# First layer's first block in whole float32 products; its weights are split later, for the second block

## Chip, core and metric

The kernel runs on one core of a Trainium2 chip. The metric is the device time of one execution in microseconds (us). TensorE (PE) multiplies, VectorE (DVE) and ScalarE (ACT) do the elementwise work, GpSimd (POOL) does almost nothing, and SyncE (SP) issues nearly all transfers.

## What is computed

A linear attention with a complex decay over 768 positions (4 batches, 8 heads of 48), and behind it two layers of a feed-forward network over 3072 tokens of 384 features, with 2048 hidden features each. The input of the first layer is the attention's output.

```python
for t in range(S):
    new_re = ar * S_re - ai * S_im
    new_im = ar * S_im + ai * S_re
    S_re, S_im = (new_re + k[t] ⊗ v[t], new_im)
    y[t] = q[t] · S_re
h = x @ w_in;  g = max(h, 0) + log1p(exp(-|h|));    x = g @ w_out     # first layer
h = x @ w_in2; g = h * tanh(softplus(h));           out = g @ w_out2  # second layer
```

## The kernel before

**Work.** The tokens are 24 units of 128. For each unit the attention runs through a decay path, sums over the positions (products with the triangular `mask`, the tiles `cum` and `pa`), a `trig` step and `heads`. Three units form a block of 384 tokens of the first layer; there are 8 such blocks, and 6 blocks of 512 in the second layer. A block goes through 16 slots, one for each chunk `f` of 128 hidden features. In the text slots 0 to 15 are the first block, 16 to 31 the second.

**Split numbers.** The products are made in the form float32r. Each operand is held as a high and a low part, and each product is made three times: high by high, low by high, high by low. The input `x` of a block gets its parts in `heads` (ACT writes the high one, DVE the low one). A slot of the first layer (`mlp`) makes nine products into the PSUM tile `h` (three pieces of 128 features, three times each), then g in eight elementwise steps on ACT and DVE (tiles `rt`), splits g into `rhi` (a cast) and `rlo` (a subtraction on DVE), and `products` makes nine products more, three into each of three accumulators `acc`.

**Weights.** `w_prep` brings one chunk of raw 64-bit numbers into a ring of two buffers (`wr`; the first two chunks have buffers in `x`), puts float32 together in four elementwise passes, casts the high part into the tile `w` and subtracts for the low part. The 16 chunks are prepared before and during the first block, each ahead of the slot that needs it, and stay for all eight blocks. Then the second layer's chunks replace them.

**Order.** A planner in the kernel (`Recorder.schedule`) takes each operation's priority (`prio`, in slots) and a cost and writes one fixed order for each engine. Operations of the kind `Flex` may go to DVE or ACT, and the planner picks which; so a change at one place moves others. `warm` fills gaps that the planner sees on PE up to the slot `WARM` = 7 with filler products of `mask` by itself (tile `idle`), at first all gaps, from slot 0 on those above 1.5 us.

Of the kernel before, what the change touches and what calls it, by code (L numbers as in the profile page):

```python
# [17 lines left out]
DM = H * D  # L18
# [411 lines left out]
class Engine:  # L430
# [16 lines left out]
    def cost(self, method, k):  # L447
        if method == "preload_act_table_set":
            return 1.283, 0.0
        out = k.get("out")  # L450
        n = out.size() if isinstance(out, View) else 0
        if method == "dma_start":
            v = min((v for v in (out, k["in_"]) if isinstance(v, View)), key=lambda v: v.size())
            return (1.0 if self.name == "pool" else 0.62), max(v.size() * 4 * (v.box[0][1] - v.box[0][0]) / 350e3, 0.5)
        if self.name == "act":
            ps = any(isinstance(v, View) and v.h.pool.psum for v in k.values())
            wide = any(isinstance(v, View) and v.h.dt == I32 for v in k.values())
            return (0.00094 if wide else 0.000833) * n + (0.051 if ps else 0.093) + (0.093 if "accum_out" in k else 0.0) + (0.093 if isinstance(k.get("bias"), View) else 0.0), 0.0
        if self.name == "dve":
            ps = any(isinstance(v, View) and v.h.pool.psum for v in k.values())  # L460
            fast = method in ("tensor_scalar", "tensor_copy") and not ps
            return (0.00052 if fast else 0.00104) * n + 0.068, 0.0
        if self.name == "pool" and method == "copy":
            return 0.00107 * n + 0.07, 0.0
        if self.name == "pool":
            return 0.0023 * n + 0.07, 0.0
        if self.name == "pe":
            rhs = k["rhs"].size()
            if k["rhs"].h.dt == F32R:
                return max(0.000414 * rhs + 0.0143, 0.107), 0.0  # L470
            if rhs == 128 and k["lhsT"].size() <= 64:
                return 0.116, 0.0
            if rhs > 128:
                return 0.001684 * rhs, 0.0
            if rhs <= 64:
                return 0.167, 0.0
            return 0.223, 0.0
        raise AssertionError(method)


def emit(tc, ri, qk, vp, w1, w2, outT, fit):
# [46 lines left out]
    def f32(v):  # L528
        return v.bitcast(F32)
# [21 lines left out]
    pool.memset(out=hpi, constant=math.pi / 2)  # L551


    W = {}


    spare = {}
    for u, f in GUESTS.items():
        spare[u] = {}
        for i, part in enumerate(PARTS):  # L560
            w, o = wp.tile((P, 4, DM), F32, f"w{f - i}"), 0
            for tag, n in part:
                spare[u][tag] = w[:, o:o + n] if n > 1 else w[:, o]
                o += n

    def w_prep(layer, f, prio, raw=None):
        rec.prio = prio
        w = wp.tile((P, 2, 2 * DM), F32R, f"w{f}")
        if raw is None:
            raw = ring1.tile((P, 2 * DM, 2), I32, "wr", bufs=WR)  # L570
        sp.dma_start(out=raw.rearrange("p b t -> p (b t)"), in_=(w1, w2)[layer - 1][f].bitcast(I32))
        lw, hw = raw[:, :, 0], raw[:, :, 1]
        wact.scale(out=f32(hw), in_=f32(hw), scale=2.0 ** -112)
        av.top3(out=lw, in_=lw)
        dve.scalar_tensor_tensor(out=lw, in0=hw, scalar=-(2 ** 31), in1=lw, op0=ALU.bitwise_and, op1=ALU.bitwise_or)
        dve.scalar_tensor_tensor(out=lw, in0=hw, scalar=3, in1=lw, op0=ALU.logical_shift_left, op1=ALU.bitwise_or)
        avp.copy(out=w[:, 0], in_=f32(lw))
        vp2.tt(out=w[:, 1], in0=f32(lw), in1=f32(w[:, 0]), op=ALU.subtract)
        for i, kind in enumerate("io"):
            W[layer, kind, f] = (w[:, 0, i * DM:(i + 1) * DM], w[:, 1, i * DM:(i + 1) * DM])  # L580


    unit_blk = {}
# [94 lines left out]
    def heads(u, t, ed, cs):  # L678
# [74 lines left out]
            xblk[j] = ring1.tile((P, NJ + 1, 2, 3 * P), F32R, "x", 2)  # L753
        x = xblk[j]
        o = slice(i0 * P, (i0 + 1) * P)
        act.activation(out=x[:, :, 0, o], in_=y, func=AF.Copy, accum_out=flags[:, u, 3:4])
        dve.tensor_tensor(out=x[:, :, 1, o], in0=y, in1=f32(x[:, :, 0, o]), op=ALU.subtract)
        if i0 == BLOCKS1[j] - 1:
            for i in range(6):
                s0 = 16 * i if i < 3 else 64 + 16 * (i - 3)  # L760
                d0 = 48 + 64 * (i % 2)
                sp.dma_start(out=f32(x[d0:d0 + 16, i // 2, :, 0:nb]), in_=f32(x[s0:s0 + 16, NJ, :, 0:nb]))


    class Slot:
# [19 lines left out]

    def mlp(s):
        n = s.n
        hi, lo = W[s.layer, "i", s.f]
        x = xblk[s.j] if s.layer == 1 else x2blk[s.j]
        rec.prio = s.i  # L790
        h = ps.tile((P, 512), F32, "h", BANKS)[:, 0:n]
        with rec.group("pe"):
            k = 0
            for wt, xi in ((hi, 0), (lo, 0), (hi, 1)):
                for j in range(NJ):
                    mm(h, wt[:, j * P:(j + 1) * P], x[:, j, xi, 0:n], k == 0, k == 8)
                    k += 1
        if chain:
            rec.ops[-1].extra = (chain.pop(),)
        chain.append(rec.ops[-1])  # L800
        rec.prio = s.i - L_ELEMENTWISE
        if s.layer == 1:
            t1, t2 = rt(s, "t1", 3), rt(s, "t2", 2)
            av.abs(out=t1, in_=h)
            act.activation(out=t1, in_=t1, func=AF.Exp, scale=-1.0)

            act.activation(out=t2, in_=t1, func=AF.Identity, bias=1.0)
            dve.scalar_tensor_tensor(out=t2, in0=t2, scalar=1.0, in1=t1, op0=ALU.subtract, op1=ALU.subtract)
# [12 lines left out]
        dve.tensor_scalar(out=z, in0=hs, scalar1=20.0, scalar2=None, op0=ALU.min)
        act.activation(out=z, in_=z, func=AF.Exp)
        act.activation(out=z, in_=z, func=AF.Ln, scale=0.5, bias=1.0)
        dve.tensor_tensor(out=z, in0=z, in1=hs, op=ALU.add)
        batch.append((s, hs, z))
        if len(batch) < VISIT:
            return
        rec.prio = s.i - L_VISIT
        with rec.group("act"):
            act.preload_act_table_set("sigmoid_and_others")  # L830
            for _, _, z in batch:
                act.activation(out=z, in_=z, func=AF.Sigmoid)
            act.preload_act_table_set("natural_log_exp_and_others")
        for r, g, z in batch:
            rec.prio = r.i - L_GATE
            ghi, glo = rt(r, "hi", 4, F32R), rt(r, "lo", 4, F32R)
            dve.tensor_tensor(out=g, in0=g, in1=z, op=ALU.mult)
            av.copy(out=ghi, in_=g)
            dve.tensor_tensor(out=glo, in0=g, in1=f32(ghi), op=ALU.subtract)
            products(r, ghi, glo)  # L840
        batch.clear()

    def products(s, ghi, glo):
        n = s.n
# [6 lines left out]
        for e in range(NJ):  # L851
            o = slice(e * P, (e + 1) * P)
            with rec.group("pe"):
                mm(a[e][:, 0:n], hi[:, o], ghi, first, False)
                mm(a[e][:, 0:n], lo[:, o], ghi, False, False)
                mm(a[e][:, 0:n], hi[:, o], glo, False, last)
            if last:
                if s.layer == 1:
                    t = rt(s, "ev", 2)
                    av.copy(out=t, in_=a[e][:, 0:n])  # L860
                    sp.dma_start(out=x2d[e, :, s.t0:s.t0 + n], in_=t)
                else:
# [318 lines left out]
```

## Time and profile before

| | us |
|---|---|
| median of 3 runs (1054.78 to 1057.41) | 1055.84 |
| the profiled execution's own time | 1053.35 |
| its span from first to last instruction | 1051.6 |
| first product of slot 0 | 64.2 |
| first product of slot 16 | 160.3 |
| first product of slot 32 | 233.7 |
| PE busy in the span | 1017.9 |
| DVE busy | 921.5 |
| ACT busy | 875.3 |

A busy time is the union of an engine's records. The records of PE are longer than the distance between two products, since a product starts while the one before it is still in the array, and the fillers count as busy too. The records of DVE and ACT overlap a little in the same way. So the text takes the cost of an instruction from the distance between two starts where it can.

### The profile page before, as it was taken

What the parts mean: (1) busy time and instruction counts of PE and PEld (TensorE: products, weight loads), DVE (VectorE), ACT (ScalarE), POOL (GpSimd) and SP (SyncE); (2) the same over time, 40 slices, a digit from 0 to 9 for tenths busy, and PEclk for the clock granted to TensorE, in tenths of its full rate; (3) what the DMA queues carried; (4) which work ended last, traced back from release to release, by engine and by line L of the source; (5) the groups of instructions that cost most, each with busy time, mean ns of one, the idle gap of its engine ahead of it and who ended that gap; (6) DMA issues with size and microseconds to landing.
All of it is one profiled execution on the core that took longest, in us unless ns stands there. A gap on an engine that the chain in (4) does not pass through costs nothing.

```text
span 1051.6 us, 17036 instructions
## 1 busy us (share of the span) xinstructions
PE 1017.9 (97%) x6022; PEld 911.3 (87%) x6022; DVE 921.5 (88%) x1680; ACT 875.3 (83%) x1639; POOL 16.4 (2%) x28
## 2 busy tenths in 40 slices
PE   9999879999999999999999999789999999999997
PEld 8898778999999999999999998568888888888886
DVE  7999999999999999999998999898877687776764
ACT  8987989889889888898986789659888877788883
POOL 0000000000000000000000000000000000000000
PEclk9999999999999999999999999899999999999999
DMA  6157453344434444444334323221010100000000
GB/s 265 46 162 215 148 162 89 81 94 100 94 83 99 98 86 95 86 98 97 68 73 102 112 94 112 90 91 41 21 31 31 30 31 1 1 31 1 31 1 33
DMA packets 158791, 84.69 MB, mean 81 GB/s; under 512 B 136916, under 2 KB 139988, under 8 KB 158696
## 3 DMA queue, kind: packets, MB, share of 16 engines
q1 hardware_dynamic: 158056, 83.45, 29.7%
q8 instruction: 49, 0.80, 0.3%
q14 instruction: 46, 0.38, 0.1%
q0 software_dynamic: 640, 0.06, 0.1%
HBM read 55.11 MB, written 9.50 MB: 61 GB/s over the span
## 4 chain that ended last, share of the span: by engine, by line
PE 81%; DVE 8%; ACT 6%; DMA 3%; issue 1%; SPq 0%; DVEq 0%; ACTq 0%
PE acc L986 34%; PE h L986 34%; PE pa L986 7%; PE cum L986 5%; DMA wr<-w 2%; DVE rt L992 2%; DVE wr L992 2%; ACT rt L992 1%; ACT L982 1%; PE idle L986 1%; ACT w L992 1%; DVE w L992 1%; DVE rlo L992 1%; ACT wr L966 0%; DMA w<-ri 0%
## 5 line engine op out<-in xcount | busy, mean ns | idle before, releaser
L986 PE MATMUL h<-x,w 128*128 128x384 f32 (+1 forms) x2016 | 435.9, 362 | 10.0 <-DVE w L990 6.2
L986 PEld LDWEIGHTS h<-x,w 128*128 128x128 f32 x2016 | 366.3, 190 | 47.4 <-DVE w L990 7.0
L992 ACT ACTIVATE rt<-rt 128x384 f32<-128x384 f32 (+1 forms) x672 | 361.0, 565 | 51.5 <-DVE rt L992 44.4
L986 PE MATMUL acc<-rhi,w 128*128 128x384 f32 (+1 forms) x1344 | 383.3, 366 | 3.2 <-ACT rhi L988 2.2
L986 PEld LDWEIGHTS acc<-rhi,w 128*128 128x128 f32 x1344 | 246.0, 189 | 34.2 <-ACT rhi L988 4.2
L986 PE MATMUL acc<-rlo,w 128*128 128x384 f32 (+1 forms) x672 | 242.5, 361 | 1.4 <-DVE rlo L992 1.3
L992 DVE TENSOR_TENSOR rt<-rt,rt 128x512 f32<-128x512 f32 (+1 forms) x320 | 196.9, 633 | 22.1 <-ACT rt L992 20.1
L982 ACT ACT_TABLE_LOAD x115 | 147.5, 1283 | 2.8 <-PEq L1164 0.8
L986 PEld LDWEIGHTS acc<-rlo,w 128*128 128x128 f32 x672 | 126.7, 188 | 15.9 <-DVE rlo L992 4.7
L992 DVE TENSOR_TENSOR rlo<-rt,rhi 128x384 fp32r<-128x384 f32 (+1 forms) x224 | 136.0, 610 | 4.6 <-ACT rhi L988 3.0
L988 ACT CAST rhi<-rt 128x384 fp32r<-128x384 f32 (+1 forms) x158 | 86.4, 548 | 28.0 <-DVE rt L992 21.4
L992 DVE SCALAR_TENSOR_TENSOR rt<-h,rt 128x384 f32<-128x384 f32 x128 | 69.0, 552 | 0.5
L992 DVE SCALAR_TENSOR_TENSOR rt<-rt,rt 128x384 f32<-128x384 f32 x128 | 68.6, 549 | 0.7 <-ACT rt L992 0.4
L992 DVE TENSOR_SCALAR rt<-rt 128x512 f32<-128x512 f32 x96 | 40.8, 426 | 29.9 <-ACT rt L988 28.4
L979 ACT ACTIVATE rt<-h 128x384 f32<-128x384 f32 x92 | 44.6, 486 | 21.3 <-DVE rlo L992 10.4
L992 DVE SCALAR_TENSOR_TENSOR wr<-wr 128x768 int32<-128x768 int32 x58 | 55.2, 956 | 1.0 <-ACT wr L966 1.0
L990 DVE COPY rt<-h 128x512 f32<-128x512 f32 x49 | 33.8, 690 | 23.9 <-PE h L986 23.3
L986 PE MATMUL pa<-qkT 96*128 96x128 f32 x384 | 49.1, 278 | 4.9 <-DVE qt L992 1.6
L986 PEld LDWEIGHTS pa<-qkT 96*128 96x128 f32 x384 | 46.4, 191 | 7.5 <-DVE qt L992 2.0
L988 ACT COPY rt<-h 128x512 f32<-128x512 f32 x47 | 27.5, 586 | 28.4 <-PE h L986 27.9
L986 PEld LDWEIGHTS idle<-mask 128*128 128x128 f32 x388 | 46.8, 198 | 3.6 <-DVE mask L990 1.7
L986 PE MATMUL idle<-mask 128*128 128x128 f32 x388 | 47.7, 282 | 1.7 <-DVE mask L990 1.7
(115 smaller groups left out, 985.8 us busy)
## 6 DMA issues: line engine op xcount, KB each, us to landing
wr<-w SPq DMA_DIRECT2D x29, 768.0 KB, 4.2
qkT<-st SPq DMA_DIRECT2D x252, 64.0 KB, 2.3
ri<-ri SPq DMA_DIRECT2D x22, 384.0 KB, 3.1
qkin<-qk SPq DMA_DIRECT2D x22, 384.0 KB, 3.5
v<-vp SPq DMA_DIRECT2D x24, 256.0 KB, 3.6
x2d<-rev SPq DMA_DIRECT2D x24, 192.0 KB, 2.1
x2r<-x2d SPq DMA_DIRECT2D x6, 768.0 KB
outT<-rev SPq DMA_DIRECT2D x18, 256.0 KB, 2.0
```

The lines of the kernel that those rows point to most:

```text
L979: eng.activation(out=o, in_=i, func=AF.Abs)
L982: eng.preload_act_table_set(*a)
L986: eng.matmul(res(k["out"]), lhsT=res(k["lhsT"]), rhs=res(k["rhs"]), start=k["start"], stop=k["stop"])
L988: eng.copy(res(k["out"]), res(k["in_"]))
L990: eng.tensor_copy(res(k["out"]), res(k["in_"]))
L992: getattr(eng, method)(*[res(v) for v in a], **{n: res(v) for n, v in k.items()})
```

## The change

In the first block neither x nor g is split, and a product is made once in whole float32, with whole weights: three products instead of nine into `h`, three instead of nine into `acc`. `w_prep` of the first layer ends with the whole chunk. A new function `split` makes the high and low parts from the whole chunk; it is called after each slot of the first block with a priority 8 slots before the slot of the second block that needs it. High and low parts have tiles of their own now, and the low part of chunk `f` takes the place of the whole chunk `f - 1`. The six transfers that complete x carry one part instead of two for the first block. The planner's cost of a product with `mask` seen as float32 rises with this.

```diff
+WHOLE = 16
+L_SPLIT = 8.0
...
-            if k["rhs"].h.dt == F32R:
+            if k["rhs"].h.dt == F32R and not any(c[0] == "bitcast" for c in k["rhs"].chain):
...
+        if layer == 1:
+            whole[f] = wp.tile((P, 2 * DM), F32, f"w{f}a")
+            dve.scalar_tensor_tensor(out=whole[f].bitcast(I32), in0=hw, scalar=3, in1=lw, op0=ALU.logical_shift_left, op1=ALU.bitwise_or)
+            return
         dve.scalar_tensor_tensor(out=lw, in0=hw, scalar=3, in1=lw, op0=ALU.logical_shift_left, op1=ALU.bitwise_or)
-        avp.copy(out=w[:, 0], in_=f32(lw))
-        vp2.tt(out=w[:, 1], in0=f32(lw), in1=f32(w[:, 0]), op=ALU.subtract)
+        split(layer, f, f32(lw))
+
+    def split(layer, f, w):
+
+        hi = wp.tile((P, 2 * DM), F32R, f"w{f}b")
+        lo = wp.tile((P, 2 * DM), F32R, f"w{f - 1}a" if f else "w")
+        avp.copy(out=hi, in_=w)
+        vp2.tt(out=lo, in0=w, in1=f32(hi), op=ALU.subtract)
...
-        act.activation(out=x[:, :, 0, o], in_=y, func=AF.Copy, accum_out=flags[:, u, 3:4])
-        dve.tensor_tensor(out=x[:, :, 1, o], in0=y, in1=f32(x[:, :, 0, o]), op=ALU.subtract)
+        if NF * j < WHOLE:
+            act.activation(out=f32(x[:, :, 0, o]), in_=y, func=AF.Copy, accum_out=flags[:, u, 3:4])
...
+            if s.i < WHOLE:
                 for j in range(NJ):
-                    mm(h, wt[:, j * P:(j + 1) * P], x[:, j, xi, 0:n], k == 0, k == 8)
-                    k += 1
+                    mm(h, whole[s.f][:, j * P:(j + 1) * P], f32(x[:, j, 0, 0:n]), j == 0, j == NJ - 1)
...
+            if s.i < WHOLE:
+                g = rt(s, "hi", 2, F32R)
+                dve.tensor_tensor(out=f32(g), in0=t1, in1=t2, op=ALU.add)
+                products(s, g, None)
+                return
...
+                if glo is None:
+                    mm(a[e][:, 0:n], whole[s.f][:, DM + e * P:DM + (e + 1) * P], f32(ghi), first, last)
...
+        if WHOLE - NF <= s.i < WHOLE:
+            rec.prio = s.i + NF - L_SPLIT
+            split(1, s.f, whole[s.f])
```

The order on DVE around the elementwise work of the first two slots, before (`rt` are the temporaries of g, `td`, `xs`, `qt` and `st` belong to the attention):

```order
L992 SCALAR_TENSOR_TENSOR rt_734<-h,rt_734 128x384
L992 SCALAR_TENSOR_TENSOR rt_765<-rt_765,rt_739 128x384
L992 TENSOR_TENSOR rt_698<-rt_698,rt_734 128x384
L992 SCALAR_TENSOR_TENSOR rt_765<-h,rt_765 128x384
L990 CAST rhi<-rt_698 128x384
L992 TENSOR_TENSOR td<-ri 128x384
L992 TENSOR_TENSOR rlo<-rt_698,rhi 128x384
L977 TENSOR_SCALAR rt_866<-h 128x384
```

and the same place of the change:

```order
L1026 SCALAR_TENSOR_TENSOR rt_723<-h,rt_723 128x384
L1026 SCALAR_TENSOR_TENSOR rt_783<-rt_783,rt_738 128x384
L1026 TENSOR_TENSOR rhi<-rt_711,rt_723 128x384
L1026 SCALAR_TENSOR_TENSOR rt_783<-h,rt_783 128x384
L1026 TENSOR_TENSOR td<-ri 128x384
L1011 TENSOR_SCALAR rt_811<-h 128x384
L1024 CAST w6b<-w6a 128x768
L1024 CAST w7b<-w7a 128x768
```

The sum that makes g writes `rhi` itself, the cast and the subtraction are gone, and two casts of the later split of weights stand already here.

DVE at the end of the first block, where the last slots' g is made and the third unit of the second block comes near, before:

```order
L992 TENSOR_TENSOR rt_1592<-rt_1592,rt_1652 128x384
L992 TENSOR_TENSOR tab<-tab,tc 128x384
L992 TENSOR_SCALAR ri<-ri 128x384
L992 SCALAR_TENSOR_TENSOR tc<-tab,tc 128x384
L992 TENSOR_TENSOR rt_1669<-rt_1669,rt_1686 128x384
L992 TENSOR_TENSOR tc<-td,tc 128x384
L992 TENSOR_TENSOR rlo<-rt_1592,rhi 128x384
L992 TENSOR_TENSOR rlo<-rt_1669,rhi 128x384
L992 SCALAR_TENSOR_TENSOR rt_1755<-rt_1755,rt_1692 128x384
```

and of the change:

```order
L1026 TENSOR_SCALAR ri<-ri 128x384
L1026 SCALAR_TENSOR_TENSOR tc<-tab,tc 128x384
L1026 TENSOR_TENSOR rhi<-rt_1357,rt_1407 128x384
L1026 TENSOR_TENSOR tc<-td,tc 128x384
L1026 TENSOR_TENSOR qt<-pa,mask 128x512
L1026 SCALAR_TENSOR_TENSOR rt_1441<-h,rt_1441 128x384
L1026 TENSOR_TENSOR st<-pa,mask 128x512
L1026 TENSOR_TENSOR w5a<-w6a,w6b 128x768
L1026 SCALAR_TENSOR_TENSOR rt_1490<-rt_1490,rt_1436 128x384
L1026 TENSOR_TENSOR w6a<-w7a,w7b 128x768
```

The subtractions `rlo` are gone and those of the weights (`w5a<-w6a,w6b` is the low part of chunk 6, `w6a<-w7a,w7b` that of chunk 7) stand between the elementwise steps. The step with `rt_1490` is slot 16's; ahead of it eight of the 16 chunks are split, the other eight come behind it.

PE at the products of slot 0 into `acc` (`w_266` and `w0a` are chunk 0, `w_366` and `w1a` chunk 1; `cum` and `pa` are attention), before:

```order
L986 MATMUL acc<-rhi,w_266 128x384 x2
L986 MATMUL acc<-rlo,w_266 128x384
L986 MATMUL cum<-qt,v 64x128 x4
L986 MATMUL cum<-st,v 64x128 x4
L986 MATMUL pa<-v,kt 96x48 x8
L986 MATMUL acc<-rhi,w_266 128x384 x2
L986 MATMUL acc<-rlo,w_266 128x384
L986 MATMUL acc<-rhi,w_266 128x384 x2
L986 MATMUL acc<-rlo,w_266 128x384
L986 MATMUL idle<-mask 128x128 x33
L986 MATMUL acc<-rhi,w_366 128x384 x2
```

and of the change:

```order
L1020 MATMUL acc<-rhi,w0a 128x384
L1020 MATMUL cum<-qt,v 64x128 x4
L1020 MATMUL cum<-st,v 64x128 x4
L1020 MATMUL pa<-v,kt 96x48 x8
L1020 MATMUL acc<-rhi,w1a 128x384
L1020 MATMUL acc<-rhi,w0a 128x384 x2
L1020 MATMUL acc<-rhi,w1a 128x384 x2
L1020 MATMUL idle<-mask 128x128 x14
L1020 MATMUL cum<-xs,mask 128x384
L1020 MATMUL acc<-rhi,w2a 128x384 x3
```

Each accumulator gets one product instead of three, and 33 fillers between chunks 0 and 1 become 14 behind chunk 1. In the whole program the fillers go from 194 to 149. Up to slot 108 the orders differ in many single places, since the planner chooses anew; from there to the end the order on PE, DVE and ACT is the same.

## Rows read from the trace of the kernel before

**Rows 1.** The page: busy time of the engines, and the granted clock in 40 slices

```profile
PE 1017.9 (97%) x6022; PEld 911.3 (87%) x6022; DVE 921.5 (88%) x1680; ACT 875.3 (83%) x1639; POOL 16.4 (2%) x28
...
PEclk9999999999999999999999999899999999999999
```

**Rows 2.** Busy time by stretch; after the length PE, PEld, DVE, ACT, POOL, clock

```profile
64.00:110.00 46.00, 43.02 (x334) 39.53 (x334) 45.44 (x76) 38.28 (x76) 1.66 (x2) 1.00 0.68 190
110.00:160.00 50.00, 41.54 (x243) 38.41 (x242) 48.56 (x83) 44.90 (x84) 1.51 (x2) 0.93 0.50 148
160.00:235.00 75.00, 73.65 (x503) 68.59 (x502) 73.31 (x139) 66.58 (x148) 2.27 (x3) 1.00 0.41 90
235.00:550.00 315.00, 314.00 (x2195) 298.53 (x2194) 301.43 (x586) 278.79 (x610) 9.84 (x13) 1.00 0.41 90
550.00:650.00 100.00, 100.00 (x581) 96.63 (x580) 94.01 (x179) 79.67 (x155) 0.00 (x0) 1.00 0.37 113
650.00:710.00 60.00, 49.35 (x186) 35.67 (x185) 54.44 (x87) 38.57 (x55) 0.00 (x0) 0.91 0.23 80
```

**Rows 3.** The same view for the filler products (tile idle) alone: PE, PEld

```profile
64.00:110.00 46.00, 15.15 (x130) 14.91 (x129) 1.00 0.68 190
110.00:160.00 50.00, 0.38 (x2) 0.36 (x2) 0.93 0.50 148
```

**Rows 4.** Timeline of PE: start, length, what, count (columns as in the heading)

```profile
72.33 0.81 PE L986 MATMUL cum<-xs,mask 128*128 128x384 f32 x2
72.98 0.81 PE L986 MATMUL pa<-xs,mask 128*128 128x384 f32 x2
73.62 5.08 PE L986 MATMUL idle<-mask 128*128 128x128 f32 x44
78.45 1.81 PE L986 MATMUL h<-x,w 128*128 128x384 f32 x9
...
114.47 1.72 PE L986 MATMUL h<-x,w 128*128 128x384 f32 x9
116.03 0.51 PE L986 MATMUL acc<-rhi,w 128*128 128x384 f32 x2
```

**Rows 5.** The same timeline, two waits of PE in the first block

```profile
124.26 2.84 PE L986 MATMUL h<-x,w 128*128 128x384 f32 x9 [1.82 <-DVE rt L992]
...
146.86 1.56 PE L986 MATMUL pa<-v,kt 128*96 128x48 f32 x16 [2.53 <-DVE x L992]
```

**Rows 6.** Groups of DVE, 64 to 176 us; columns: busy us, mean ns, idle before

```profile
L992 DVE TENSOR_TENSOR w<-wr,w 128x768 fp32r<-128x768 f32 x11 | 10.5, 951 | 0.5 <-ACT w L988 0.4
...
L992 DVE TENSOR_TENSOR rlo<-rt,rhi 128x384 fp32r<-128x384 f32 x16 | 8.8, 553 | 0.2 <-ACT rhi L988 0.2
...
L992 DVE TENSOR_TENSOR x<-cum,x 128x512 fp32r<-128x512 f32 x3 | 2.1, 685 | 0.0
L990 DVE CAST rhi<-rt 128x384 fp32r<-128x384 f32 x5 | 1.8, 354 | 0.0
L990 DVE CAST w<-wr 128x768 fp32r<-128x768 f32 x3 | 1.7, 556 | 0.0
L977 DVE TENSOR_SCALAR rt<-h 128x384 int32<-128x384 int32 x3 | 1.7, 555 | 0.0
```

**Rows 7.** Groups of DVE over the whole span, same columns

```profile
L964 DVE TENSOR_SCALAR wr<-wr 128x768 int32<-128x768 int32 x8 | 4.5, 557 | 0.0
...
L990 DVE COPY qkT<-h 96x512 f32<-96x512 f32 x3 | 2.0, 680 | 0.2 <-PE h L986 0.2
```

**Rows 8.** Timeline of DVE

```profile
101.53 1.02 DVE L992 SCALAR_TENSOR_TENSOR rt<-rt,rt 128x384 f32<-128x384 f32 x2
102.46 0.68 DVE L992 TENSOR_TENSOR qt<-pa,mask 128x512 f32<-128x512 f32 x1
```

**Rows 9.** Groups of ACT over the whole span, same columns as rows 6

```profile
L988 ACT CAST rhi<-rt 128x384 fp32r<-128x384 f32 x97 | 49.2, 507 | 22.2 <-DVE rt L992 16.9 <-PE acc L986 2.8 <-PE h L986 1.5
...
L988 ACT CAST w<-wr 128x768 fp32r<-128x768 f32 x19 | 17.1, 901 | 2.2 <-DVE wr L992 2.2
```

More of the change, by code (lines that the diff above doesn't have):

```diff
@@ L551, in emit @@
     pool.memset(out=hpi, constant=math.pi / 2)
-    W = {}
+    W, whole = {}, {}
     spare = {}
@@ L560, in emit @@
         for i, part in enumerate(PARTS):
-            w, o = wp.tile((P, 4, DM), F32, f"w{f - i}"), 0
+            w, o = None, 0
             for tag, n in part:
-                spare[u][tag] = w[:, o:o + n] if n > 1 else w[:, o]
+                if o % 2 == 0:
+                    w = wp.tile((P, 2, DM), F32, f"w{f - i}" + "ab"[o // 2])
+                spare[u][tag] = w[:, o % 2:o % 2 + n] if n > 1 else w[:, o % 2]
                 o += n
@@ L567, in w_prep @@
         rec.prio = prio
-        w = wp.tile((P, 2, 2 * DM), F32R, f"w{f}")
         if raw is None:
@@ L575, in w_prep @@
         dve.scalar_tensor_tensor(out=lw, in0=hw, scalar=-(2 ** 31), in1=lw, op0=ALU.bitwise_and, op1=ALU.bitwise_or)
+        if layer == 1:
+            whole[f] = wp.tile((P, 2 * DM), F32, f"w{f}a")
+            dve.scalar_tensor_tensor(out=whole[f].bitcast(I32), in0=hw, scalar=3, in1=lw, op0=ALU.logical_shift_left, op1=ALU.bitwise_or)
+            return
         dve.scalar_tensor_tensor(out=lw, in0=hw, scalar=3, in1=lw, op0=ALU.logical_shift_left, op1=ALU.bitwise_or)
-        avp.copy(out=w[:, 0], in_=f32(lw))
-        vp2.tt(out=w[:, 1], in0=f32(lw), in1=f32(w[:, 0]), op=ALU.subtract)
+        split(layer, f, f32(lw))
[4 more added lines that the diff above has]
+        vp2.tt(out=lo, in0=w, in1=f32(hi), op=ALU.subtract)
         for i, kind in enumerate("io"):
-            W[layer, kind, f] = (w[:, 0, i * DM:(i + 1) * DM], w[:, 1, i * DM:(i + 1) * DM])
+            W[layer, kind, f] = (hi[:, i * DM:(i + 1) * DM], lo[:, i * DM:(i + 1) * DM])
     unit_blk = {}
@@ L755, in heads @@
         o = slice(i0 * P, (i0 + 1) * P)
-        act.activation(out=x[:, :, 0, o], in_=y, func=AF.Copy, accum_out=flags[:, u, 3:4])
-        dve.tensor_tensor(out=x[:, :, 1, o], in0=y, in1=f32(x[:, :, 0, o]), op=ALU.subtract)
+        if NF * j < WHOLE:
+            act.activation(out=f32(x[:, :, 0, o]), in_=y, func=AF.Copy, accum_out=flags[:, u, 3:4])
+        else:
+            act.activation(out=x[:, :, 0, o], in_=y, func=AF.Copy, accum_out=flags[:, u, 3:4])
+            dve.tensor_tensor(out=x[:, :, 1, o], in0=y, in1=f32(x[:, :, 0, o]), op=ALU.subtract)
         if i0 == BLOCKS1[j] - 1:
@@ L761, in heads @@
                 d0 = 48 + 64 * (i % 2)
-                sp.dma_start(out=f32(x[d0:d0 + 16, i // 2, :, 0:nb]), in_=f32(x[s0:s0 + 16, NJ, :, 0:nb]))
+                parts = slice(0, 1) if NF * j < WHOLE else slice(0, 2)
+                sp.dma_start(out=f32(x[d0:d0 + 16, i // 2, parts, 0:nb]), in_=f32(x[s0:s0 + 16, NJ, parts, 0:nb]))
     class Slot:
@@ L787, in mlp @@
         n = s.n
-        hi, lo = W[s.layer, "i", s.f]
         x = xblk[s.j] if s.layer == 1 else x2blk[s.j]
@@ L792, in mlp @@
         with rec.group("pe"):
-            k = 0
-            for wt, xi in ((hi, 0), (lo, 0), (hi, 1)):
+            if s.i < WHOLE:
                 for j in range(NJ):
-                    mm(h, wt[:, j * P:(j + 1) * P], x[:, j, xi, 0:n], k == 0, k == 8)
-                    k += 1
+                    mm(h, whole[s.f][:, j * P:(j + 1) * P], f32(x[:, j, 0, 0:n]), j == 0, j == NJ - 1)
+            else:
+                hi, lo = W[s.layer, "i", s.f]
+                k = 0
+                for wt, xi in ((hi, 0), (lo, 0), (hi, 1)):
+                    for j in range(NJ):
+                        mm(h, wt[:, j * P:(j + 1) * P], x[:, j, xi, 0:n], k == 0, k == 8)
+                        k += 1
         if chain:
@@ L844, in products @@
         n = s.n
-        hi, lo = W[s.layer, "o", s.f]
+        if s.i >= WHOLE:
+            hi, lo = W[s.layer, "o", s.f]
         if s.f == 0:
@@ L853, in products @@
             with rec.group("pe"):
-                mm(a[e][:, 0:n], hi[:, o], ghi, first, False)
-                mm(a[e][:, 0:n], lo[:, o], ghi, False, False)
-                mm(a[e][:, 0:n], hi[:, o], glo, False, last)
+                if glo is None:
+                    mm(a[e][:, 0:n], whole[s.f][:, DM + e * P:DM + (e + 1) * P], f32(ghi), first, last)
+                else:
+                    mm(a[e][:, 0:n], hi[:, o], ghi, first, False)
+                    mm(a[e][:, 0:n], lo[:, o], ghi, False, False)
+                    mm(a[e][:, 0:n], hi[:, o], glo, False, last)
             if last:
```

## Prediction

> **What bounds the kernel now.** I read the page first, then busy times by stretch, then the timelines of PE and DVE. The page says PE, 97% busy [rows 1]. That figure holds fillers and overlapping records, so I went on by stretch. From 64 to 160 us, the first block, PE's records cover 43.02 + 41.54 = 84.6 of 96 us, but 15.15 + 0.38 = 15.5 of these are fillers [rows 2, 3]. Real work covers 69.0. DVE covers 45.44 + 48.56 = 94.0 of the same 96, with nothing in it that could be left out, and ACT 83.2 [rows 2]. PE waits there for DVE: 1.82 us for a temporary of g, 2.53 us for x [rows 5]. So the first block is bound by DVE. From 235 to 550 us PE has 314.0 of 315 and DVE 301.4 [rows 2]: both are full, and nobody gives the other much room. From 550 to 650 PE is full and DVE at 94.0, at the change of layers (650 to 710) both stall in places [rows 2].
>
> The consequence for any change to the first block: what DVE is relieved of there comes out as time, as long as PE fits. Since PE and DVE are full in every later stretch, a lead won by 235 us is kept to the end, and not made larger.
>
> **What the change takes from DVE.** Records of DVE overlap: two steps of 384 columns start at 101.53 and the next instruction at 102.46, that is 0.465 each, while the mean record of such a step is 0.553 [rows 6, 8]. I take 0.087 off every record.
> Gone: 16 subtractions `rlo`, 16 x (0.553 - 0.087) = 7.46 us; three subtractions for the low part of x, 3 x (0.685 - 0.087) = 1.79 [rows 6]. Together 9.25.
> The planner's new choices, counted over both orders: DVE loses five casts of `rhi` (0.267 each, 1.34), three absolute values (0.468, 1.40) and two casts of weights (0.469, 0.94) [rows 6]; it gains five copies of the transposed tile from PSUM (0.593, 2.97), four passes over raw weights (0.470, 1.88) [rows 7] and two copies of the attention's state, which DVE has not in the trace and which I put between a cast of `rhi` and such a copy, at the absolute value's 0.47 (0.27 to 0.59 each, 0.94). Net 2.1 back.
> The splits of weights are only moved: 16 subtractions of 0.951 each [rows 6] before and after. They leave the time before slot 16 for eight chunks, 8 x 0.864 = 6.9 us, and come back in the second block.
> Sum on DVE: 9.25 - 2.1 = **7.1 us less** in all, and up to 14 less at the start of slot 16, of which half returns.
>
> **ACT** loses eleven casts of `rhi` at 0.507 and gains two casts of weights at 0.901 [rows 9], 3.8 less by the records; its other exchanges with DVE are the mirror of those above and add about 4 less (nine fewer passes and copies, three more absolute values; an estimate by the durations of DVE for the same work, 9 x 0.6 - 3 x 0.55). So ACT is relieved by as much as DVE and does not become the bound.
>
> **What it puts on PE.** A whole float32 product of 384 columns takes 0.645 us: `cum` starts at 72.33, `pa` at 72.98, the filler at 73.62 [rows 4]. Nine split products start at 114.47 and the next at 116.03: 0.173 each [rows 4]. The first block has 96 products of three parts: 96 x (0.645 - 3 x 0.173) = **12.1 us more**. That price is read off products with `mask` as the weight, where I have no row for 384 columns with changing weights. Below it could not go by any row; above it, a full record of 0.81 us for the two halves of a product [rows 4] would make the term 28 us, if nothing of a product overlapped with the next. I keep 0.645, since there the next product, with another operand, starts behind it at that distance; the high end goes into rival 4. In exchange 45 fillers go (194 to 149); 22 of them take from 73.62 to 78.45, 0.22 each [rows 4], 9.9 us. Fillers are cover and cost nothing where they are, so this is no gain; it says that PE's planned gaps shrink by nearly what the products grow.
> Does it fit? PE's real 69.0 us and 12.1 make 81.1, in 96 less the 7.5 of the forecast, 88.5: 7.4 us are left for waits. Narrow, but it fits.
> The Trainium skill says in FP8 and Floating Point Precision, TensorE Precision Notes, that true float32 makes four passes through the array. By that a whole product would be 4 x 0.173 = 0.692 and the term 16.6 us instead of 12.1, with 2.9 us left in place of 7.4; the row says 3.7 passes, and the sum goes by the row.
>
> The transfers that complete x are half as large, and the raw ring comes free one cast and one subtraction earlier (0.469 + 0.864 us of DVE, if DVE does both [rows 6]). I count both at nothing, since DVE's own load covers them: a chunk that lands earlier still waits for its passes on a full DVE. Without that cover it would be a gain.
>
> **Sum.** 7.1 us of DVE in a stretch where DVE is busy 94.0 of 96, so 7.1 x 96/94 = 7.3, and a little for ACT's relief: 7.5. The profiled execution took 1053.35, its span 1051.6 with 1.75 around it: 1053.35 - 7.5 = 1045.85. The median of the runs shown is 2.49 above that execution, so the forecast is 1055.84 - 7.5 = **1048.3 us**. A measurement of this kernel can tell about 0.3%, 3.2 us, from no change.
>
> **Rivals.**
> 1. *A larger gain.* Before slot 16 the eight later splits (6.9 us) are still out. If PE takes that lead and the second block has room for them, in waits that now stand in 160 to 235 us (DVE 73.31 of 75, so 1.7 us) and in DVE's slack further on (13.6 us of 315 [rows 2]), about 4 us more is kept: 1055.8 - 11.5 = 1044.3. For it: DVE has 4% slack after 235 us. Against: PE has none there.
> 2. *The splits are felt in the second block.* DVE is full there, and slot 16 + f cannot start before chunk f is split. If the planner's eight slots of lead are eaten, PE waits where it never waited before, some 0.5 us in each of eight slots: 4 us back, 1052.3. Decides if DVE's split subtractions stand right before the products that read them.
> 3. *PE takes the place of DVE.* If PE's waits are latency (product, ACT, DVE, product) and not DVE's load, they stay, and the longer products come on top, less the fillers' 9.9: +12.1 - 9.9 = 2.2, 1058.0. For it: 97% on the page. Against: DVE's 94.0 of 96.
> 4. *Slower.* From 110 us on there are only 0.38 us of fillers [rows 3], and nine slots (7 to 15) are computed there: 9 x 6 x 0.126 = 6.8 us more work on PE in a stretch that has waits and no filler to give up. If the waits do not shrink there, it is 1055.8 + 6.8 = 1062.6. The clock works the same way: the granted mean is 0.93 there over 50 us [rows 2], so 3.5 us of the high level were given up; behind the wait of 1.82 us nine products take 2.84 us, elsewhere 1.72 [rows 4, 5]. It decides from the point where waits and slow clock together take more than the 7.4 us that are left; the high end of a whole product's price would do it alone.
> The Trainium skill says in TensorE: Matmul & The Clock Gate, HAM oscillation, that gaps without work bring TensorE's clock back to its low level, anew each time. The trace agrees where it has waits (0.93). By that rule fewer fillers between slots 0 and 7 could bring a second loss of that size, and the time would be 1062.6 + 3.5 = 1066.1.
>
> **How the numbers follow.** Forecast 0.50 (its own range 1044.8 to 1051.5, an allowance of some 3 us for the many places where the planner's order differs), rival 1 0.15, rival 2 0.13, rival 3 0.13, rival 4 0.09. Rivals 1 and the forecast are faster by over 3.2 us; rival 2 is on the edge, half each: faster 0.70, less some doubt of the forecast's upper end, 0.68. Same: half of rival 2, and rival 3 (2.2 us is within 3.2): 0.21. Slower: rival 4 and the upper part of 3, 0.11. The range takes in rival 1 with 1 us below and rival 2, and goes to the lower part of rival 3: 1043 to 1057.5.
>
> **What would show it.** After the change DVE should still be busy over 95% from 64 us to slot 16, with 16 fewer `rlo` and whole sums into `rhi`; slot 16 should begin 9 to 12 us earlier than 160.3, slot 32 (now 233.7) some 7 to 9; products with `w0a` to `w15a` should start 0.64 to 0.65 apart; 45 fillers fewer. The stretch of the change of layers should look the same, 7 to 8 us earlier. I am wrong if PE's idle time between slots 7 and 16 grows or stays, if the clock's 0.93 falls further, or if PE waits for `w` in the second block.

## The result, and the profile after

The change ran at 1046.55 us, median of 4 runs (1045.53 to 1047.30), beside 1055.94 for the kernel before on the same chip: ratio 0.991, interval 0.9893 to 0.9927, that is 9.5 us less. It was measured twice more on other chips, 0.9928 (0.9905 to 0.9951) and 0.9905 (0.9889 to 0.992), so 7.6 and 10.0 us less; the mean of the three gains is **9.0 us**. The prediction said 7.5. The profiled execution took 1045.53, its span 1043.8.

The page of the change, against [rows 1]:

```profile
PE 1017.8 (98%) x5836; PEld 885.9 (85%) x5836; DVE 912.6 (87%) x1662; ACT 866.9 (83%) x1622; POOL 16.9 (2%) x28
...
PEclk9999999999999999999999999889999999999999
```

DVE has 8.9 us less, where 7.1 was expected; a busy time is a union, so the overlap of the records is already out of it. Part of the difference is that records of one kind are shorter: an `rlo` has a mean of 0.547 us in the change, 0.553 before. ACT has 8.4 less (about 8 expected). PE's sum stands still, since its longer products took the place of fillers.

Busy time by stretch (columns as in [rows 2]; the first two stretches are the first block up to slot 16 and the second up to slot 32), before:

```profile
64.00:160.20 96.20, 84.76 (x575) 78.06 (x575) 94.20 (x159) 83.25 (x159) 3.18 (x4) 0.96 0.58 168
160.20:233.60 73.40, 72.05 (x494) 67.08 (x493) 71.71 (x135) 65.22 (x146) 2.27 (x3) 1.00 0.41 91
```

and of the change:

```profile
64.00:148.00 84.00, 81.38 (x408) 53.06 (x407) 82.76 (x140) 74.17 (x147) 3.71 (x4) 1.00 0.65 186
148.00:222.00 74.00, 73.70 (x484) 65.62 (x483) 72.87 (x133) 65.36 (x142) 2.27 (x3) 1.00 0.39 86
222.00:550.00 328.00, 324.34 (x2250) 307.94 (x2249) 313.80 (x606) 288.04 (x630) 9.85 (x13) 1.00 0.41 89
550.00:650.00 100.00, 99.38 (x565) 93.80 (x563) 93.64 (x178) 80.64 (x151) 0.00 (x0) 1.00 0.33 105
650.00:702.00 52.00, 42.47 (x152) 31.42 (x152) 46.63 (x73) 30.67 (x45) 0.00 (x0) 0.87 0.28 92
```

The first block takes 84 us instead of 96. DVE fills it as before (82.76 of 84, 98.5%), PE nearly does too (81.38), and the clock that was 0.93 from 110 to 160 us [rows 2] is 1.00. Of PE's 81.38, 5.72 are fillers by the same view for them alone, against 15.5 before [rows 3]:

```profile
64.00:148.00 84.00, 5.72 (x47) 5.52 (x46) 1.00 0.65 186
```

The waits of PE from 64 to 222 us (what PE waited for: us in total, times, longest):

```profile
PE pa L1020 <- DVE rt L1011: 0.9, 1, 0.9
PE h L1020 <- DVE rt L1026: 0.9, 2, 0.7
PE acc L1020 <- DVE rhi L1026: 0.4, 1, 0.4
PE acc L1020 <- DVE S L1024: 0.3, 1, 0.3
PE pa L1020 <- DVE rt L1026: 0.2, 1, 0.2
```

That is 2.7 us in both blocks. The waits of 1.82 and 2.53 us [rows 5] are gone, and in no line is a tile of weights what PE waited for.

PE's timeline of the change (start, length, what; a whole product has two records):

```profile
67.66 2.10 PE L1020 MATMUL h<-x,w1a 128*128 128x384 f32 x6
69.60 2.10 PE L1020 MATMUL h<-x,w2a 128*128 128x384 f32 x6
71.53 0.81 PE L1020 MATMUL cum<-xs,mask 128*128 128x384 f32 x2
...
88.54 3.29 PE L1020 MATMUL idle<-mask 128*128 128x128 f32 x28
91.72 0.91 PE L1020 MATMUL cum<-xs,mask 128*128 128x384 f32 x2
93.06 2.20 PE L1020 MATMUL acc<-rhi,w2a 128*128 128x384 f32 x6 [0.42 <-DVE rhi L1026]
...
147.94 0.98 PE L1020 MATMUL h<-x,w0b 128*128 128x384 f32 x3
...
221.72 0.68 PE L1020 MATMUL h<-x,w0b 128*128 128x384 f32 x3
```

Three whole products with changing weights start at 67.66 and the next three at 69.60: 1.94 / 3 = 0.647 each, the next three 1.93 / 3 = 0.643. Slot 16 begins at 147.94 instead of 160.3 and slot 32 at 221.72 instead of 233.7: both 12 us earlier. By slot 104 only 8.3 of these are left, and that lead stays to the end.

### The profile page after: what moved, and what is told of

Read it like the earlier page. It is cut to its first block, busy times and chain, and to the rows that moved or that the text cites. A ratio compares the mean times of both kernels' runs of the same rounds, so it can differ in the third digit from the quotient of the medians.

```text
span 1043.8 us, 16617 instructions
## 1 busy us (share of the span) xinstructions
PE 1017.8 (98%) x5836; PEld 885.9 (85%) x5836; DVE 912.6 (87%) x1662; ACT 866.9 (83%) x1622; POOL 16.9 (2%) x28
## 4 chain that ended last, share of the span: by engine, by line
PE 76%; DVE 13%; DMA 4%; SPq 3%; ACT 2%; issue 2%; DVEq 0%
PE h L1020 31%; PE acc L1020 31%; PE pa L1020 7%; PE cum L1020 5%; DVE rt L1026 3%; SPq L1026 3%; DMA wr<-w 2%; DVE wr L1026 2%; DVE rlo L1026 1%; PE idle L1020 1%; DMA qkT<-st 1%; DVE st L1026 1%; DVE xs L1026 1%; DMA w10a<-ri 1%; DVE qt L1026 0%
## 5 line engine op out<-in xcount | busy, mean ns | idle before, releaser
L1026 DVE TENSOR_TENSOR rlo<-rt,rhi 128x384 fp32r<-128x384 f32 (+1 forms) x208 | 126.6, 611 | 5.9 <-ACT rhi L1022 3.5
L1013 ACT ACTIVATE rt<-h 128x384 f32<-128x384 f32 x95 | 46.1, 486 | 25.3 <-DVE rlo L1026 12.6
L1020 PEld LDWEIGHTS pa<-qkT 96*128 96x128 f32 x384 | 45.7, 191 | 10.6 <-issue 6.5
L1026 DVE SCALAR_TENSOR_TENSOR wr<-wr 128x768 int32<-128x768 int32 x44 | 41.8, 954 | 0.5 <-ACT wr L1000 0.4
L1020 PEld LDWEIGHTS idle<-mask 128*128 128x128 f32 x298 | 37.4, 204 | 3.9 <-DVE mask L1024 1.7
L1020 PE MATMUL idle<-mask 128*128 128x128 f32 x298 | 38.4, 288 | 1.7 <-DVE mask L1024 1.7
L1024 DVE CAST rhi<-rt 128x512 fp32r<-128x512 f32 (+1 forms) x61 | 23.7, 392 | 12.3 <-PE acc L1020 11.9
L1020 PE MATMUL cum<-qkT,S 96*48 96x128 f32 x320 | 34.0, 272 | 0.0
L1026 ACT ACTIVATE tab<-ri 128x768 f32<-128x768 f32 (+1 forms) x44 | 29.7, 675 | 4.2 <-DVE xs L1026 2.3
L1020 PEld LDWEIGHTS pa<-v,kt 128*96 128x96 f32 x288 | 25.8, 164 | 3.3 <-issue 3.3
L1020 PE MATMUL pa<-v,kt 128*96 128x48 f32 x288 | 28.0, 250 | 0.0
L1020 PE MATMUL h<-x,w13b 128*128 128x384 f32 (+1 forms) x78 | 21.2, 382 | 3.2 <-DVE w13b L1024 3.2
```

Of the source, the lines that this page charges most:

```text
L1013: eng.activation(out=o, in_=i, func=AF.Abs)
L1020: eng.matmul(res(k["out"]), lhsT=res(k["lhsT"]), rhs=res(k["rhs"]), start=k["start"], stop=k["stop"])
L1024: eng.tensor_copy(res(k["out"]), res(k["in_"]))
L1026: getattr(eng, method)(*[res(v) for v in a], **{n: res(v) for n, v in k.items()})
```

## The experiments

The theory was the prediction's: the load of DVE in the first block sets the time there, and the lead is kept, since PE is full from the second block on. Against it stood four others: that the splits' later place, not the removed work, makes the gain; that ACT is as near the bound as DVE; that PE's products set the time; and that the fillers, through the clock, decide it. In the table, "gain" is the time of before on the same chip times one less the ratio. The last columns say how much earlier (-) a slot's first product starts than in the profile of before; these are single executions, and three of the change itself differ by up to 4 us. e1 to e4 ran on a chip without the change beside them and are held against the mean of its three gains, 9.0 (7.6 to 10.0); a loss read from them is uncertain by some 2 us.

| kernel | median us (runs) | ratio, interval | gain us | slot 16 | 32 | 56 | 104 | 200 |
|---|---|---|---|---|---|---|---|---|
| the change | 1046.55 (4) | 0.991, 0.9893 to 0.9927 | 9.5 | -12.3 | -11.9 | -12.3 | -8.3 | -8.1 |
| the change again (e8) | 1049.59 (6) | 0.9928, 0.9905 to 0.9951 | 7.6 | -10.8 | -10.4 | -10.8 | -4.4 | -3.8 |
| the change a third time (e12) | 1047.67 (4) | 0.9905, 0.9889 to 0.992 | 10.0 | -11.1 | -10.7 | -11.1 | -7.1 | -6.2 |
| early splits (e1) | 1051.47 (8) | 0.9956, 0.994 to 0.9973 | 4.7 | -3.4 | -5.1 | -4.7 | -1.2 | -2.8 |
| late splits (e7) | 1050.59 (6) | 0.9936, 0.9918 to 0.9954 | 6.8 | -9.0 | -7.9 | -6.5 | -3.2 | -3.4 |
| more on DVE (e2) | 1051.82 (8) | 0.9957, 0.9942 to 0.9972 | 4.5 | -9.8 | -7.0 | -7.3 | -4.4 | -4.9 |
| more on ACT (e3) | 1047.34 (6) | 0.9931, 0.9909 to 0.9952 | 7.3 | -9.9 | -10.0 | -10.3 | -7.6 | -6.3 |
| more on PE (e4) | 1051.90 (6) | 0.9957, 0.9942 to 0.9972 | 4.5 | +3.9 | -2.8 | -1.4 | 0.0 | 0.0 |
| two blocks whole (e5) | 1053.67 (12) | 0.9968, 0.9956 to 0.9981 | 3.4 | -12.5 | +6.3 | -0.8 | -1.3 | -1.9 |
| no late fillers (e6) | 1042.28 (5) | 0.9864, 0.9844 to 0.9885 | 14.4 | -11.1 | -10.6 | -10.4 | -9.0 | -8.3 |
| the same again (e10) | 1044.29 (4) | 0.9883, 0.9867 to 0.9898 | 12.4 | -12.8 | -12.3 | -12.4 | -11.5 | -12.4 |
| same order, no late fillers (e9) | 1044.82 (4) | 0.9887, 0.9872 to 0.9903 | 11.9 | -10.1 | -9.8 | -10.1 | -8.5 | -8.8 |
| before, no late fillers (e11) | 1057.28 (12) | 1.0001, 0.9991 to 1.0012 | -0.1 | +2.5 | +3.2 | +2.5 | +3.0 | +2.7 |

### The place of the splits: e1 and e7

All splits early, 18 slots ahead of their need instead of 8, so that most of the splits lie in the first block again:

```diff
-L_SPLIT = 8.0
+L_SPLIT = 18.0
```

> The weights are split early: the priority of each split is 10 slots earlier, so that nearly all 16 stand in the first block; the rest is the change. Theory A (VectorE's load in the first block sets the time until TensorE is full, and a lead is kept from there): VectorE has 6 us more to do before slot 16 than in the change and the same in all, so slot 16 begins some 5.5 to 7 us before that of the kernel before instead of 12.3, slot 32 some 6 to 9 before instead of 11.9, and the time is 5 to 7 us under the kernel before (1049 to 1051). Theory B (TensorE's waits and its clock: fewer waits in the chain of a slot): the chain of a slot is as in the change, so the time is, too, 9 us under before (1047). Theory C (the gain is the deferred split alone): the gain is gone, 1055.

About half the gain is gone: 4.7 us are left. Busy time of e1 up to slot 16 and up to slot 32:

```profile
64.00:156.80 92.80, 84.17 (x429) 55.45 (x428) 89.04 (x146) 76.95 (x150) 3.18 (x4) 1.00 0.60 167
156.80:228.60 71.80, 71.80 (x483) 65.26 (x481) 71.25 (x133) 62.02 (x138) 2.27 (x3) 1.00 0.42 91
```

DVE's records up to slot 16 shrank from 94.20 to 89.04, 5.2 us, while its gaps grew from 2.0 to 3.8 us (of 96.2 before and 92.8 now), and slot 16 is only 3.4 us earlier. The longest of these gaps is the edit's own: the low part of chunk 6 takes the place of the whole chunk 5, and DVE waits until PE has made the products with that chunk:

```profile
123.83 0.96 DVE L1026 TENSOR_TENSOR w5a<-w6a,w6b 128x768 fp32r<-128x768 f32 x1 [1.48 <-PE acc L1020]
```

The subtractions of the splits, in DVE's timelines of both (two of each, at slot 16's start and behind it), first the change:

```profile
147.73 0.95 DVE L1026 TENSOR_TENSOR w3a<-w4a,w4b 128x768 fp32r<-128x768 f32 x1
151.21 0.95 DVE L1026 TENSOR_TENSOR w4a<-w5a,w5b 128x768 fp32r<-128x768 f32 x1
```

and e1:

```profile
156.73 0.95 DVE L1026 TENSOR_TENSOR w11a<-w12a,w12b 128x768 fp32r<-128x768 f32 x1
162.38 0.96 DVE L1026 TENSOR_TENSOR w12a<-w13a,w13b 128x768 fp32r<-128x768 f32 x1
```

At the start of slot 16 the change (147.94) has only begun to subtract for chunk 4, so 12 chunks are still out, 12 x 0.864 = 10.4 us of DVE; e1 (156.8) is at chunk 12, so 4 are out, 3.5 us. So 6.9 us of subtractions lie between the two, and 9.0 - 4.7 = 4.3 us of time; the wait of 1.48 us, which the change does not have, may be part of that difference. That the later place counts is shown; its exact price is not.

The other direction, 4 slots ahead:

```diff
-L_SPLIT = 8.0
+L_SPLIT = 4.0
```

> The splits four slots later than in the change, so that more of them stand in the second block (VectorE's work before slot 16 is 4 us less than in the change, before slot 32 4 us more). Theory A (what counts is the lead when TensorE becomes full): slot 16 begins about 15 us before that of the kernel before, slot 32 only 7 to 9, and the time is 5 to 8 us under before (1048 to 1051). Rival (the later the better): 11 us or more under before.

6.8 us against 7.6 for the change on the same chip: no further gain, and the intervals overlap. Slot 16 came only 9.0 us earlier, less than in the change, though more splits lay behind it. The clock's mean from 64 to 110 us was 0.96 there, which the change does not show, and the planner put 2.7 us more on DVE (915.3 on its page against 912.6). Whether the shorter lead or one of these brought it down is open.

### More work on one engine at a time: e2, e3, e4

Each adds, in every slot of the first block, one instruction whose result nobody reads. On DVE a subtraction of 384 columns, 16 x 0.465 = 7.4 us before the planner's other choices:

```diff
+                dve.tensor_tensor(out=rt(s, "lo", 2, F32R), in0=t1, in1=f32(g), op=ALU.subtract)
                 products(s, g, None)
```

> In each slot of the first block VectorE does one subtraction of 384 columns more, whose result nobody reads (the removed one put back as load alone); the planner moves three passes over raw weights and three absolute values from VectorE to ScalarE in return, so that VectorE has 5 us more than in the change. Theory A: slot 16 begins 5 to 7 us before that of the kernel before instead of 12.3, and the time is 4 to 5 us under before (1051 to 1052). Theory B: nobody waits for the extra work, the chain of a slot is unchanged: 9 us under before (1047).

4.5 us of the gain are lost. But the planner moved six other passes from DVE to ACT and one cast the other way, so the load that was put on DVE is not 7.4 us. The page of e2 has DVE at 917.0, where the change has 912.6:

```profile
PE 1016.5 (97%) x5850; PEld 885.4 (85%) x5850; DVE 917.0 (88%) x1673; ACT 870.0 (83%) x1627; POOL 16.4 (2%) x28
```

That is 4.4 us more on DVE for 4.5 us of time: one for one, as far as a loss uncertain by 2 us can tell. Busy time of e2 up to about slot 16 (150.4) and up to shortly before slot 32 (226.7):

```profile
64.00:150.00 86.00, 81.86 (x415) 54.17 (x414) 84.47 (x144) 75.97 (x150) 3.18 (x4) 1.00 0.64 181
150.00:226.00 76.00, 73.65 (x480) 64.94 (x479) 75.29 (x139) 65.37 (x142) 2.27 (x3) 1.00 0.38 85
```

On ACT a copy in the same place:

```diff
+                act.activation(out=rt(s, "lo", 2, F32R), in_=f32(g), func=AF.Copy)
                 products(s, g, None)
```

> In each slot of the first block ScalarE makes one copy of 384 columns more, whose result nobody reads: 16 times about 0.5 us, 8 us of ScalarE, which gives its earlier casts back as load; VectorE's work is that of the change within 0.5 us. Theory A: ScalarE covers 76.2 of 86 us from 64 to 150 us in the change, so 8 us nearly fit: slot 16 begins 10 to 12 us before that of the kernel before and the time is 7 to 9 us under it (1047 to 1049). Rival (ScalarE's relief is what counts as much as VectorE's): 2 to 4 us under before (1052 to 1054).

Gain 7.3, 1.7 less than the mean of the change and within what its three measurements differ by. On the page ACT has 5.1 us more than in the change (872.0 against 866.9) and DVE the same:

```profile
PE 1019.1 (97%) x5836; PEld 887.2 (85%) x5836; DVE 912.6 (87%) x1663; ACT 872.0 (83%) x1637; POOL 16.4 (2%) x28
```

So ACT is not as near the bound as DVE, though the intervals of e2 and e3, on the same chip, overlap by 0.001. On PE one whole product more, into the tile of the fillers, 16 x 0.645 = 10.3 us:

```diff
+                    if j == 0:
+                        mm(idle[:, 0:n], whole[s.f][:, 0:P], f32(x[:, 0, 0, 0:n]), True, True)
```

> In each slot of the first block TensorE makes one whole product of 384 columns more, whose result nobody reads: 16 x 0.645 = 10.3 us. Theory A, with the room that the prediction left for TensorE (7.4 us): part of it fits, slot 16 begins 7 to 9 us before that of the kernel before and the time is 4 to 6 us under it (1050 to 1052). Theory D (TensorE is as full as VectorE in the first block of the change): all of it comes out, the time is that of the kernel before or 1 us more (1056 to 1057). If TensorE has much more room than was worked out: 9 us under before.

4.5 us are lost. They are not PE's alone: the planner also moved work from ACT to DVE, whose page shows 2.4 us more than the change's (915.0). Busy time of e4 up to slot 16:

```profile
64.00:164.00 100.00, 96.42 (x493) 62.63 (x491) 96.22 (x162) 88.01 (x171) 3.64 (x5) 1.00 0.60 166
```

Slot 16 is 16 us later than in the change, more than was added, and slot 32 still 2.8 us earlier than before: the planner had placed more of other work ahead of slot 16. The start of one slot alone misleads here; slot 32 and the ratio do not.

### The second block whole too: e5

```diff
-WHOLE = 16
+WHOLE = 32
```

> The first two blocks in whole products, the splits of weights one block later; otherwise the change. TensorE gets 12.1 us more in the second block, VectorE and ScalarE lose as much there as in the first; the planner moves 15 casts and 11 copies to VectorE in return, so that VectorE's sum is 2 us under the change's and ScalarE's far under. Theory A with TensorE full from the second block on: the relief finds no room, slot 32 begins 0 to 4 us before that of the kernel before instead of 11.9, and the time is 2 us under to 3 us over the kernel before (1055 to 1060). Rival (whole products pay wherever VectorE is nearly full): slot 32 begins over 15 us earlier and the time is 13 us or more under before.

The gain shrinks to 3.4 us, somewhat more than the 2 at most that were expected. Busy time from slot 16 to slot 32 of e5:

```profile
148.00:240.00 92.00, 91.99 (x497) 61.77 (x495) 88.74 (x157) 71.08 (x149) 3.09 (x4) 1.00 0.45 96
```

PE has no idle time at all there, and the block takes 92 us instead of 74. The first block leads by the same 12.5 us; in the second PE takes DVE's place, though DVE, relieved, gives a part back later (slot 32 is 6.3 us late, slot 56 again 0.8 early). So in this kernel the change is worth its price in the first block, where PE had fillers and waits, and not in the second.

### The fillers: e6, e9, e10, e11

In e6 `warm` fills gaps up to slot 0 alone, not up to slot 7:

```diff
-        if s.i in (0, WARM):
+        if s.i == 0:
```

> The change without the 15 fillers after slot 0. Theory A: fillers lie in gaps and cost nothing, so the time is that of the change, 8 to 10 us under before (1047), if the clock stays at its high level between slots 0 and 16. Rival (fewer fillers bring falls of the clock in the first block, the prediction's fourth rival): at least one fall between 64 and 150 us, and 1.5 to 4 us of the gain are lost.

It was faster than the change: gain 14.4. But the planner also chose another order. So e9 takes the late fillers out of the finished order and leaves every other instruction where the change has it (149 fillers become 135), and e10 and e12 ran beside it:

```diff
-            if t is not None and (first or op.t - t > 1.5):
+            if t is not None and first:
```

> The change with the order of every engine kept and only the 14 fillers behind chunk 1 left out (the one that the planner places itself stays). e6 came out 14 us under before, 7 more than the change on the same chip. Theory F (fillers on TensorE hold real products up): this one gains as much, 12 to 15 us under before. Theory O (the gain of e6 comes from its other order, or from the PSUM bank that the filler held to slot 7): this one is like the change, 7 to 9.5 us under.

> e6 again: if it is 12 us or more under before once more, it is a better version; if it is 8 to 10, the first result was the spread of single executions (the change's ran from 1045.5 to 1053.6 in one set).

> The change once more beside e9 to e11: 7.5 to 9.5 us under before.

e6 and the change beside it (e8) are clearly apart, 0.9864 (up to 0.9885) and 0.9928 (from 0.9905). On the other chip e9 gained 11.9 and e10 12.4, the change beside them 10.0; there the intervals overlap by 0.0014 and 0.0009. By its size e9's gain is near theory F, but e11 below speaks against it. PE's timeline of e9 at the place where the change has its 14 fillers:

```profile
87.87 1.45 PE L1020 MATMUL acc<-rhi,w1a 128*128 128x384 f32 x4
92.34 1.65 PE L1020 MATMUL cum<-xs,mask 128*128 128x384 f32 x2 [3.02 <-DVE rt L1026]
93.78 3.46 PE L1020 MATMUL acc<-rhi,w2a 128*128 128x384 f32 x5
```

and the busy time of e9 around it:

```profile
64.00:110.00 46.00, 41.08 (x210) 26.80 (x209) 43.65 (x76) 37.48 (x76) 1.66 (x2) 0.93 0.60 170
```

Behind the wait of 3.02 us `cum` takes 1.65 instead of 0.91: the granted clock fell, to a mean of 0.93 in this stretch, where it is 1.00 in the change. Slot 16 came 1 us later than in the change on the same chip (e12). Still the kernel ended no later. In e10, with its other order, the clock stayed at 1.00 in this stretch without the late fillers, in e6 its mean was 0.96.

The same edit in the kernel before (194 fillers become 131):

> The kernel before without the fillers after slot 0 (63 fewer). Theory F: it gains 4 us or more on the kernel before. Theory O and theory A (fillers lie in gaps): within 3 us of it, and if the clock falls between 64 and 110 us, up to 3 us more.

Ratio 1.0001: nothing, where theory F wanted 4 us or more. Its clock had a mean of 0.81 in the same stretch:

```profile
64.00:110.00 46.00, 33.96 (x193) 28.94 (x193) 42.49 (x70) 35.46 (x70) 1.66 (x2) 0.81 0.65 185
```

### Where the lead goes back between slots 56 and 104

The change on the chip a second time, to see whether the loss of lead is the kernel's or one execution's:

> The change itself, on the chip of e5 to e7, for comparison: 8 to 10.5 us under before.

All three executions of the change lose 4 to 6.4 us between these slots, e9 1.6, e10 0.9, e6 1.4. The waits of PE from 235 to 560 us in the change:

```profile
PE pa L1020 <- DMA qkT<-st: 2.9, 4, 1.5
PE pa L1020 <- issue: 0.8, 2, 0.6
```

The kernel before has 1.0 us of waits in the same window and none for `qkT<-st`, the 12 transfers that transpose q and k for a unit. e8 has 3.6 of these, e12 2.0, e9 0.5, e10 0.5, e6 0.7. PE's timeline of the change has one of 1.51 us:

```profile
347.87 2.02 PE L1020 MATMUL pa<-qkT 96*128 96x128 f32 x16 [1.51 <-DMA qkT<-st]
```

The issues of that unit's transfers on SP in the change (how long one took in ns, least, median and most; then the first and last start):

```profile
L1026 SPq DMA_DIRECT2D qkT<-st x12: 602/627/1950, 336.5 to 345.2; - x12
```

The DMA queues of the change from 338 to 340 us (packets, MB, share of the engines):

```profile
q8 instruction: 1, 0.02, 5.0%
```

The issues of the same unit in e9, where PE's wait for it is 0.19 us:

```profile
L1026 SPq DMA_DIRECT2D qkT<-st x12: 601/627/629, 338.7 to 346.1; - x12
```

In the change one of the 12 issues takes 1.95 us instead of 0.627, just when a packet of instructions is loaded, and PE waits 1.51 us instead of 0.19, as much longer as that issue is too long (1.95 - 0.63 = 1.3). e8 and e12 have the same at the same unit (2.04 and 2.01, with the packet beside it); e6, e9 and e10 have no long issue there (632, 629 and 632 ns at most). In e9 and e10 such a packet, and the long issue (1.46 and 1.52 us), lie in the next unit's issues, some 25 us later. Long issues are no rarer there: of the 252 issues of `qkT<-st`, 5 take over 0.9 us in the change, 8 before, 7 in e9 and 6 in e10. They fall on other units.

## Why the prediction was right, step by step

- **DVE bounds the first block.** Shown in the main. DVE is 98.5% busy in the shorter block; 4.4 us more on it cost 4.5 us of time, 5.1 us more on ACT cost 1.7, which is within the spread.
- **The price of a whole product, 0.645.** Right, with changing weights too: 0.643 to 0.647. The Trainium skill's four passes (FP8 and Floating Point Precision, TensorE Precision Notes) would be 0.692; the trace shows 3.7 times the 0.173 of a split product.
- **It fits on PE.** Right, and narrower than it looked. PE's real work up to slot 16 is 81.38 - 5.72 = 75.7 of 84 us; but of the 8.3 us left 5.7 are fillers, all of them before 110 us, and 10.3 us more on PE, with 2.4 more on DVE, cost 4.5.
- **The sum on DVE, 7.1 less in all.** Measured 8.9, so the term was 1.8 too small.
- **One us on DVE is one us of time (7.1 x 96/94).** Borne out up to slot 32. From 64 us to there DVE's records are 94.20 + 71.71 = 165.9 us before, 82.76 + 72.87 = 155.6 in the change, 89.04 + 71.25 = 160.3 in e1 and about 160.4 in e2 (84.47 + 75.29 up to 226.0 and the 0.7 us behind it). That is 10.3, 5.6 and 5.5 us less, and slot 32 came 11.9, 5.1 and 7.0 us earlier.
- **The splits are only moved, worth nothing in the sum.** This term was too small. Not eight but twelve subtractions came behind slot 16's start (the prediction had counted up to slot 16's elementwise steps, later than its first product), and what they made free was kept in part: the change gains 4.3 us more than e1, which has eight of these twelve early. That is rival 1's mechanism, and nearly its price (4 us). By slot 32 all splits have been made in both kernels, and the change still leads e1 by 7 us in their profiles; DVE's records from slot 16 to 32 rose only from 71.71 to 72.87, so other work gave way there, which could be late without PE waiting for it.
- **A lead won by 235 us is kept to the end.** This step failed. In the three executions of the change the lead fell from 11.9, 10.4 and 10.7 us at slot 32 to 8.1, 3.8 and 6.2 at slot 200, nearly all of it between slots 56 and 104. PE's waits from 235 to 560 us, most of them for the transposing transfers, are 1.9 to 3.5 us above the 1.0 of before; the rest was not found.
- **Sum.** The later place of the splits (some 4 us more, an estimate from e1) and the lead given back (some 4 us less, from the profiles) both stood at nothing in the sum, and they nearly cancel. So that the total came out near is in part luck. How much of the 9.0 us the removed work alone is worth is not pinned: e1, with four of the splits late, keeps 4.7 and has the wait of 1.48 us that the change does not have.
- **Rival 2** (PE waits for split weights): none of the waits up to 222 us is for one. **Rival 3** (PE's waits are latency and stay): they fell from 12.6 us (13 lines of the waits before, of which [rows 5] has the longest two) to 2.7. **Rival 4** (clock): the clock is 1.00 from 64 to 222 us, where before it fell to 0.93. The Trainium skill's rule in TensorE: Matmul & The Clock Gate, HAM oscillation, that gaps bring the clock down again, agrees with e9 and e11 (0.93 and 0.81 once the fillers are out). The price that the rival put on a fall does not show: the ratios are 0.9887 and 1.0001.
- **What would show it.** Slot 16 came 10.8 to 12.3 us earlier (9 to 12 said), slot 32 10.4 to 11.9 (7 to 9 said, for the reason above), fillers 45 fewer in the order, 388 to 298 records in the trace. The change of layers looks the same 8 us earlier: PE 42.47 and DVE 46.63 of 52 us, before 41.47 and 46.44 from 658 to 710.

Leaving the late fillers out of the change makes a version that beats the kernel before by 14.4 us (e6) and 12.4 us (e10), 6.8 and 2.4 us more than the change beside it; in the second case the intervals overlap by 0.0009. Why is settled in part only. It is hardly the fillers' own time on PE in the first block: slot 16 came 0.3 us earlier than in the change beside it in e6, 1.7 earlier in e10, 1.0 later in e9. What the profiles show is that the lead is kept later: between slots 56 and 104 these three lose 0.9 to 1.6 us, the change 4 to 6.4. Of that the long issue that meets the unit for which PE waits explains 1.3 us. That a program shorter by 14 products moves the loads of instructions to other places is argued, not shown; and in e11 the same edit gave nothing.

## What to carry to other kernels

Where one engine bounds a stretch and another has fillers in it, trade the first one's passes for longer instructions on the second, and stop where the second is full (e5). Work that is due later can count as time, too, if it leaves the bound stretch and the next one has something else that can give way; count it by when it leaves, not only by whether it returns. Look at whether a lead that was won early is still there at the end: here 4 to 7 us of 10 to 12 were given back. And where a planner chooses the engines, read the price of an added instruction from what the engine really got: 7.4 us were put on DVE in e2, and its page shows 4.4.

## What the runs showed of the hardware that was not expected

- The issue of a transfer on SP can take 1.3 to 1.95 us instead of 0.63: 5 of the 252 issues of `qkT<-st` in the change did, each with a packet of the queue of instructions just before it. Six other such packets fell into issues and stretched none, so what decides it is open. Where SP's issues are the last wait, a long one is felt on PE (1.51 us instead of 0.19).
- With the order kept, the granted clock was 1.00 from 64 to 110 us with the late fillers and had a mean of 0.93 without them (e9), and the kernel was not slower for it: the ratios are 0.9905 (e12) and 0.9887.
